# Pooling v on VectorE from a second load, with the first loads paced and the turns reordered

## The chip, the cores and the metric

The program runs on one core of one Trainium2 chip. The metric is the device time of one execution in microseconds (us). Engines are named as in the profile: PE is TensorE (PEld its weight loads), DVE is VectorE, ACT is ScalarE, POOL is GpSimd, SP is SyncE, whose queue issues all the loads.

## What is computed

Attention over q, k, v of shape (2, 8, 576, 64) in float32, and two MLPs behind it. The attention is a sum of two parts: a local one (each query sees the keys less than 4 positions away) and a pooled one, in which q, k and v are averaged over groups of 4 positions and the result is repeated 4 times.

```python
q_d = q.reshape(B, H, Sd, factor, D).mean(axis=3)      # k_d, v_d alike; Sd = 144
out_d = sm_attn(q_d, k_d, v_d)
out_up = np.repeat(out_d, factor, axis=2)
out_local = ...                                         # |i - j| < 4, softmax, times v
return out_up + out_local
```

The sum is laid out as 1152 tokens of 512 and goes through x @ w_in, a gate, @ w_out, and then through a mixture of 4 experts with a ReLU (w1, w2), weighted by domain_probs.

## The kernel before

**Units.** The attention runs in 8 units (`Unit`, u = 0 to 7): batch u // 4, and a pair of heads hp = u % 4, whose 2 x 64 dimensions lie on the 128 partitions. Two units share one slot for k and one for q (a pair of units, 0 to 3). All big buffers are slots of 128 x 2048 float32; there are 17 (`take`, `give`).

**Loads.** SP issues, in this order: k and q of unit 0, of unit 1, then v of batch 0 (`load_v`, nine loads), then k and q of units 2 and 3 (`load_qk(1)`). v is loaded as overlapping windows, so its 576 rows of 2048 B become 1091 rows. `load_qk(2)` follows in step 1. All else is in the list `later`, from which `load_next` takes one entry at its places in steps 2 and up: the halves of the first two w_in weights, v of batch 1, k and q of the last pair. Many of those wait for a one-element memset on DVE (`hold`), which itself waits for the slot.

**One unit's work.** `sums` adds groups of four of k and q (POOL; k of units 0 and 1 on DVE, L580). `pooled_scores` (four matmuls of 72 queries each, L670), `masks` (L594) and `scores` (L607) run on PE. `pooled_softmax`, `less_max`, `normalise` and `pooled_normalise` run on DVE, ACT and POOL. `turn` (L654) and `pooled_turn` (L724, eight transposes) turn the weights, ACT copies them to SBUF (`aT`, `aTd`). `values` multiplies by v in 72 local products (L744) and by the pooled v (L755), ACT copies the pooled part (`pd`), DVE adds it to the local part (`xf`, L769), ACT writes the high part of x (L777) and `low` the rest (DVE, L785).

**Pooled v.** `pool_v(b)` makes it with matmuls of v's windows against a matrix of ones (`fours`, L463), once for each batch: in step 1 for batch 0, behind 8 idle products, and in step 5 for batch 1. ACT copies the result into the last v slot (L471).

**Order.** The loop `for t in range(NU + 2)` (L1052) writes out the order of PE, DVE, ACT and POOL by hand; each engine works through its own list in order, and so SP through its own, whose order is not written by hand. Step t holds the scores of unit t, the turns of unit t - 1 and the values of unit t - 2. `idle_products` (L551) are matmuls on zeros whose result nobody reads: 4 ahead of `pooled_scores`, 4 ahead of `turn`. PSUM has three pairs of banks that go round (`banks()`) and one more pair (`banks(True)`), which the values use.

**Behind it.** `convert` takes one step at a time of the splitting of the MLP's weights: four steps a weight on DVE (L237, L247, L259 with L268, L226) with ACT between. In steps 8 and 9 the first products of the MLP (`pieces`, `first`, L374 to L376) mix with the last units. Piece f needs weight f // 2, all three of its products; the first piece with tokens of batch 1 needs x of unit 7 (`low`, L785).

## Time and profile before

| | us |
|---|---|
| median of 3 runs | 657.13 (656.95 to 657.19) |
| the profiled execution | 657.16 |
| its span, from the first to the last instruction | 655.0 |
| attention, until PE starts step 8 | 63.5 |
| its first 18.5 us, before PE starts step 2 | 18.5 |
| PE busy, of the span | 647.4 |
| DVE busy, of the span | 415.9 |

2.2 us of the profiled execution lie outside the span. Step t is counted from where PE starts its first idle products of that step.

### The profile page before, as it was taken

To read this page: it belongs to the slowest core of one execution; us is meant where nothing else is said; L and a number is where in the kernel's file an instruction comes from. 1 tells how busy PE (TensorE), PEld (TensorE's weight loads), DVE (VectorE), ACT (ScalarE), POOL (GpSimd) and SP (SyncE) were. 2 spreads that over 40 slices of the span, in tenths; PEclk is the share of its full clock that TensorE was granted. 3 is DMA by queue.
4 is the path that set the end of the run, shared out by engine and by line. 5 is a ranking of instruction groups with operands and counts; after the bars stand their busy time and mean duration, and the time that the engine had idled before them with its cause. 6 is when DMAs were issued, how large, how long until landed. Compare 5 with 4: busy or idle time off the path is not lost.

```text
span 655.0 us, 11972 instructions
## 1 busy us (share of the span) xinstructions
PE 647.4 (99%) x4929; PEld 582.6 (89%) x4943; DVE 415.9 (63%) x839; ACT 253.3 (39%) x591; POOL 95.3 (15%) x142
## 2 busy tenths in 40 slices
PE   8999999999999999999999999999999999999997
PEld 4657999999999999998998998998998988988985
DVE  6578899852794247585665665665765665755742
ACT  5567577442554246343233232241341331331410
POOL 4762000000000062101201201201201201201000
PEclk9999999999999999999999999999999999999999
DMA  8772333300510110300110110110210300200012
GB/s 278 226 236 91 130 124 134 129 1 1 193 66 1 65 64 1 131 2 0 65 65 1 65 65 1 65 65 1 87 43 0 129 2 15 115 1 2 2 48 97
DMA packets 12147, 45.89 MB, mean 70 GB/s; under 512 B 1334, under 2 KB 3382, under 8 KB 8252
## 3 DMA queue, kind: packets, MB, share of 16 engines
q1 hardware_dynamic: 12092, 45.12, 20.3%
q8 instruction: 39, 0.64, 0.4%
q14 instruction: 16, 0.13, 0.1%
HBM read 42.76 MB, written 2.36 MB: 69 GB/s over the span
## 4 chain that ended last, share of the span: by engine, by line
PE 96%; DMA 2%; SPq 1%; issue 0%; POOL 0%; DVE 0%; POOLq 0%
PE bank L936 27%; PE bank L1205 10%; PE bank L1206 10%; PE bank L1204 10%; PE bank L374 10%; PE bank L376 10%; PE bank L375 10%; PE pair L744 2%; PE pair L551 1%; DMA slot<-in_qT_dram 1%; PE pair L755 1%; DMA slot<-in_v_dram 1%; PE pair L607 1%; PE pair L724 1%; PE pair L670 1%; PE pair L654 1%
## 5 line engine op out<-in xcount | busy, mean ns | idle before, releaser
L936 PEld LDWEIGHTS bank<-xop,slot 128*128 128x128 f32 x1344 | 180.9, 188 | 1.3
L936 PE MATMUL bank<-xop,slot 128*128 128x288 f32 x1344 | 181.8, 295 | 0.0
L1205 PE MATMUL bank<-slot,h 128*128 128x512 f32 x288 | 113.9, 395 | 0.0
L1206 PE MATMUL bank<-slot,h 128*128 128x512 f32 x288 | 113.9, 395 | 0.0
L1204 PE MATMUL bank<-slot,h 128*128 128x512 f32 x288 | 113.8, 395 | 0.0
L1212 DVE SCALAR_TENSOR_TENSOR slot<-bank,pr,slot 128x512 f32<-128x512 f32 x63 | 47.3, 751 | 85.8 <-PE bank L1206 85.8
L442 POOL TENSOR_TENSOR st<-slot 128x256 f32<-128x256 f32 x16 | 13.9, 868 | 467.4 <-DMA slot<-in_w_dram 220.5
L1206 PEld LDWEIGHTS bank<-slot,h 128*128 128x128 f32 x288 | 54.1, 188 | 13.0
L1205 PEld LDWEIGHTS bank<-slot,h 128*128 128x128 f32 x288 | 54.1, 188 | 12.4
L1204 PEld LDWEIGHTS bank<-slot,h 128*128 128x128 f32 x288 | 54.1, 188 | 12.3
L376 PE MATMUL bank<-h,slot 128*128 128x384 f32 x192 | 64.7, 337 | 0.0
L375 PE MATMUL bank<-h,slot 128*128 128x384 f32 x192 | 64.7, 337 | 0.0
L374 PE MATMUL bank<-h,slot 128*128 128x384 f32 x192 | 64.7, 337 | 0.0
L374 PE MATMUL bank<-x,slot 128*128 128x384 f32 x188 | 63.1, 336 | 0.0
L376 PE MATMUL bank<-x,slot 128*128 128x384 f32 x188 | 62.9, 335 | 0.0
L375 PE MATMUL bank<-x,slot 128*128 128x384 f32 x188 | 62.9, 335 | 0.0
L442 DVE TENSOR_TENSOR u<-bank,u 128x288 f32<-128x288 f32 x96 | 43.6, 454 | 20.4 <-PE bank L936 20.0
L965 ACT ACTIVATE h<-c 128x288 fp32r<-128x288 f32 x64 | 27.9, 445 | 71.6 <-DVE c L442 71.5
L304 ACT ACTIVATE slot<-st 128x512 fp32r<-128x512 f32 x32 | 19.2, 624 | 64.6 <-POOL st L298 64.6
L825 DVE TENSOR_TENSOR h<-slot,h 128x384 fp32r<-128x384 f32 x48 | 27.5, 585 | 24.2 <-ACT h L824 24.1
L816 ACT ACTIVATE t<-bank,half__145 128x384 f32<-128x384 f32 x47 | 27.1, 581 | 40.1 <-PE bank L376 40.1
L817 DVE SCALAR_TENSOR_TENSOR slot<-t,bank 128x384 f32<-128x384 f32 x47 | 25.8, 552 | 24.5 <-ACT t L816 24.3
(115 smaller groups left out, 920.1 us busy)
## 6 DMA issues: line engine op xcount, KB each, us to landing
slot<-in_w_dram SPq DMA_DIRECT2D x16, 1024.0 KB, 4.8
slot<-in_w_out_dram SPq DMA_DIRECT2D x8, 1024.0 KB, 4.8
slot<-in_w_in_dram SPq DMA_DIRECT2D x6, 1024.0 KB, 5.3
slot<-in_v_dram SPq DMA_DIRECT2D x6, 512.0 KB, 4.8
out_dram<-slot SPq DMA_DIRECT2D x9, 256.0 KB, 2.0
slot<-in_w_in_dram SPq DMA_DIRECT2D x4, 512.0 KB, 5.9
slot<-in_kT_dram SPq DMA_DIRECT2D x3, 576.0 KB, 5.6
slot<-in_qT_dram SPq DMA_DIRECT2D x6, 288.0 KB, 6.0
```

Source lines behind the costliest of these rows:

```text
L374: nc.tensor.matmul(ps, wh, xh, start=first, stop=False)
L375: nc.tensor.matmul(ps, wh, xl, start=False, stop=False)
L376: nc.tensor.matmul(ps, wl, xh, start=False, stop=last)
L442: eng.tensor_tensor(out=out, in0=a, in1=b, op=ALU.add)
L816: nc.scalar.activation(out=t, in_=ps, func=AF.Relu, bias=half_, scale=1.0 / (6.0 * UP))
L825: nc.vector.tensor_tensor(out=g[:, 1, :], in0=u, in1=r32(g[:, 0, :]), op=ALU.subtract)
L936: nc.tensor.matmul(ps, a[:, i, k], b[:, j, k], start=start and k == 0 and n == 0, stop=stop and k == 1 and n == 2, skip_group_check=True,)
L965: nc.scalar.activation(out=self.h[:, 0, i, j], in_=of, func=AF.Relu)
L1204: nc.tensor.matmul(ps, hh, w[:, 0], start=(f == 0), stop=False)
L1205: nc.tensor.matmul(ps, hh, w[:, 1], start=False, stop=False)
L1206: nc.tensor.matmul(ps, hl, w[:, 0], start=False, stop=(f == NF - 1))
L1212: nc.vector.scalar_tensor_tensor(out=to, in0=ps, scalar=share, in1=to, op0=ALU.mult, op1=ALU.add)
```

## The change

Pooled v is no longer made on PE. A second load (`load_four`) brings v with four neighbouring rows on one partition, and DVE adds them: for each batch a part of 128 x 4 x 256, another of the same size (the other half of the columns), and one of 16 x 4 x 512. Each part takes two adds. Accordingly the rows of pooled keys are split 128 and 16 instead of 80 and 64, and the pooled queries of two heads are grouped in three groups (80 and 80 queries, and the last 64 of each head together), so that there are three exponentials instead of four and six transposes instead of eight.

The first loads go through `load`, which makes each wait for the load that lies 1.6 MB ahead of it, until about 5.9 MB are listed. k and q of units 2 and 3 now come ahead of v; the parts of pooled v follow v; k and q of the last pair come second and third in `later`, the pooled v of batch 1 behind v of batch 1.

In units 0 and 4 (`late`) the pooled values are multiplied one step later than the local ones: ACT copies the local part, and DVE adds the pooled one to it. In step t = 3 and t = 7 `pooled_turn` stands ahead of the pooled values. The sums of k of units 2 and 3 are made on DVE. Four idle products stand between the third and the fourth product of `pooled_scores`.

```diff
-KC = PK // 2
-KR = (80, 64)
+KR = (P, PK - P)
+QG = 80
+BY_DVE = 4
+FLY = 1_600_000
+FIRST_LOADS = (3 * 2 * 2 + 4 + 4) * S * P * 4 - 1
...
+    def load(out, in_):
+        size = math.prod(in_.shape) * 4
+        dma = nc.sync.dma_start(out=out, in_=in_)
+        if sum(n for _, n in flying) > FIRST_LOADS:
+            return
+        room = FLY
+        for ins, n in reversed(flying):
+            room -= n
+            if room < 0:
+                tc.add_manual_dep(dma.ins, ins.name, DONE, reason="loads on their way")
+                break
+        flying.append((dma.ins, size))
...
-    def pool_v(b, idle=0):
-        pool = banks(True)
-        idle_products(pool, idle)
...
-                    nc.tensor.matmul(
-                        pool[g * QB : g * QB + few, r, :],
-                        fours[rows, at : at + few],
...
+    def load_four(b, part):
+        if part == 0:
+            four_slots[b] = take(), take()
+        to, cols = four(b, part)
+        if b:
+            hold(to[:, 0])
+        src = v[b].rearrange("(p f) d -> p f d", f=FACTOR)
+        load(to, src[KR[0] * (part // 2) : KR[0] + KR[1] * (part // 2), :, cols])
+
+    def pool_v(b, part):
+        f4, cols = four(b, part)
+        add(nc.vector, f4[:, :2], f4[:, :2], f4[:, 2:])
+        add(nc.vector, pooled_v(b, part // 2)[:, cols], f4[:, 0], f4[:, 1])
...
     load_qk(0, 0, 1)
     load_qk(0, 1, 1)
+    load_qk(1)
     for p in range(NP):
         load_v(0, p)
-    load_qk(1)
+    for part in range(2):
+        load_four(0, part)
...
     later = [
         lambda: load_half(0, 0),
+        lambda: load_k(NU // 2 - 1, held=True),
+        lambda: load_q(NU // 2 - 1, held=True),
         lambda: load_half(0, 1),
         lambda: load_v(1, 0, (0,)),
         lambda: load_v(1, 0, (1,)),
         lambda: load_v(1, 1, (0,)),
         last_v,
-        lambda: load_k(NU // 2 - 1, held=True),
-        lambda: load_q(NU // 2 - 1, held=True),
+        lambda: load_four(1, 0),
+        last_four,
         lambda: load_half(1, 0),
         lambda: load_half(1, 1),
     ]
```

The new order of the steps, of which the old one stands in the kernel above:

```diff
+        elif t == 1:
+            n.pooled_scores(0, 4)
+            n.masks()
+            n.scores()
+            n.pooled_softmax()
+            units[0].pooled_normalise()
+            units[2].sums_q()
+            load_qk(2)
+            load_four(0, 2)
+            n.less_max()
+            n.normalise()
+            n.pooled_normalise()
+            for m in (2, 3):
+                units[m].sums_k()
+            units[3].sums_q()
+            units[0].turn(0)
+            units[0].pooled_turn()
+        elif t == 2:
+            n.masks(4)
+            n.scores()
+            n.pooled_scores(0)
+            n.less_max()
+            load_next(t)
+            n.pooled_softmax()
+            n.normalise()
+            load_next(t)
+            n.pooled_normalise()
+            pool_v(0, 0)
+            pool_v(0, 1)
+            load_next(t)
+            units[1].turn(4)
+            units[0].values()
+            units[1].pooled_turn()
+        elif t < NU:
+            n.pooled_scores(4)
+            n.masks()
+            n.scores()
+            n.pooled_softmax()
+            load_next(t)
+            n.less_max()
+            if t == NHP:
+                units[0].low()
+            if t > 3 and t != NHP + 3:
+                units[t - 3].low()
+            if t == 3:
+                units[4].sums()
+            if t % NHP == 3:
+                pool_v(t // NHP, 2)
+            if t == NHP + 2:
+                pool_v(1, 0)
+            n.pooled_normalise()
+            n.normalise()
+            load_next(t)
+            if t < NU - 2:
+                units[t + 2].sums()
+            units[t - 1].turn(4)
+            units[t - 2].values()
+            if t % NHP == 3:
+                units[t - 1].pooled_turn()
+            if not units[t - 2].late:
+                units[t - 2].pooled_values()
+            if t % NHP == 3:
+                units[t - 3].pooled_values()
+            else:
+                units[t - 1].pooled_turn()
+            if t == NHP + 2:
+                pool_v(1, 1)
+            convert((0, 1, 2, 1, 2)[t - 3])
+            load_next(t)
```

## Rows read from the trace of the kernel before

**Rows 1.** Page: busy time of each engine over the span
```profile
PE 647.4 (99%) x4929; PEld 582.6 (89%) x4943; DVE 415.9 (63%) x839; ACT 253.3 (39%) x591; POOL 95.3 (15%) x142
```
**Rows 2.** Page: the chain that ended last, by engine
```profile
PE 96%; DMA 2%; SPq 1%; issue 0%; POOL 0%; DVE 0%; POOLq 0%
```
**Rows 3.** Stretches: length, busy time (instructions) of each engine, granted clock, DMA, GB/s
```profile
0.00:7.70 7.70, 6.41 (x93) 3.00 (x95) 3.73 (x17) 3.68 (x5) 4.12 (x23) 1.00 0.71 203
7.70:18.46 10.76, 9.37 (x148) 4.40 (x149) 6.16 (x17) 5.08 (x21) 3.92 (x7) 1.00 1.01 336
...
25.66:32.75 7.09, 6.96 (x189) 4.70 (x189) 5.16 (x16) 4.17 (x15) 4.26 (x8) 1.00 0.69 220
32.75:39.50 6.75, 6.64 (x190) 4.52 (x189) 5.73 (x17) 5.30 (x17) 4.26 (x10) 1.00 0.77 255
39.50:49.72 10.22, 10.12 (x226) 5.55 (x225) 5.98 (x16) 5.36 (x17) 7.52 (x13) 1.00 0.75 232
49.72:56.76 7.04, 6.87 (x190) 4.62 (x189) 6.03 (x15) 5.21 (x17) 1.42 (x2) 1.00 0.51 175
56.76:63.47 6.71, 6.60 (x190) 4.49 (x189) 5.58 (x14) 5.17 (x17) 1.92 (x3) 1.00 0.02 5
...
77.30:120.00 42.70, 42.70 (x249) 42.70 (x248) 42.15 (x78) 28.24 (x54) 0.00 (x0) 1.00 0.38 134
120.00:270.00 150.00, 150.00 (x859) 150.00 (x858) 86.64 (x151) 65.44 (x129) 16.92 (x16) 1.00 0.16 57
```
**Rows 4.** Timeline, start-up: start, length, engine, line, operation, idle before and releaser
```profile
11.62 0.56 PE L654 MATMUL pair<-ident,ex 64*128 64x64 f32 x10 [0.75 <-POOL ex L640]
...
16.95 1.31 POOL L442 TENSOR_TENSOR slot<-slot 128x288 f32<-128x288 f32 x3 [3.78 <-DMA slot<-in_kT_dram]
...
18.65 1.17 POOL L442 TENSOR_TENSOR slot<-slot 128x288 f32<-128x288 f32 x2 [0.39 <-DMA slot<-in_qT_dram]
...
19.88 0.71 PE L670 MATMUL pair<-slot 64*72 64x144 f32 x8 [0.38 <-POOL slot L442]
```
**Rows 5.** Timeline, PE in one whole step (t = 3)
```profile
25.66 1.03 PE L551 MATMUL pair<-zeros 128*128 128x512 bf16 x3
26.62 0.71 PE L670 MATMUL pair<-slot 64*72 64x144 f32 x8
...
29.79 1.35 PE L744 MATMUL pair<-aT,slot 38*64 38x32 f32 x72
31.08 1.21 PE L755 MATMUL pair<-aTd,slot 80*64 80x144 f32 x8
32.22 0.70 PE L724 MATMUL pair<-ident,exd 72*80 72x72 f32 x8
```
**Rows 6.** Timeline, PE: the pooling of v of batch 1 in step 5
```profile
42.06 3.64 PE L463 MATMUL pair<-slot,fours 38*32 38x512 f32 x36
```
**Rows 7.** Groups by line and shape, DVE until 78 us: count, busy, mean ns
```profile
L785 DVE TENSOR_TENSOR x<-xf,x 128x576 fp32r<-128x576 f32 x8 | 6.1, 768 | 0.2 <-ACT x L777 0.2
L683 DVE TENSOR_REDUCE mxd<-pair 72x4 f32<-72x576 f32 x8 | 5.9, 742 | 6.6 <-PE pair L670 6.5
...
L769 DVE TENSOR_TENSOR xf<-pair,pd 128x256 f32<-128x256 f32 x8 | 3.3, 415 | 0.0
...
L226 DVE TENSOR_TENSOR slot<-slot 128x512 fp32r<-128x512 f32 x4 | 2.6, 685 | 0.2 <-ACT slot L221 0.2
```
**Rows 8.** Timeline, steps 8 and 9: what the MLP's first products need from DVE
```profile
72.79 1.29 DVE L226 TENSOR_TENSOR slot<-slot 128x512 fp32r<-128x512 f32 x2 [0.18 <-ACT slot L221]
...
73.65 0.34 PE L376 MATMUL bank<-x,slot 128*128 128x384 f32 x1
...
76.98 1.42 DVE L785 TENSOR_TENSOR x<-xf,x 128x576 fp32r<-128x576 f32 x2
```
**Rows 9.** Timeline, POOL: the sums of one unit, twice
```profile
26.05 2.44 POOL L442 TENSOR_TENSOR slot<-slot 128x288 f32<-128x288 f32 x5
...
33.06 2.77 POOL L442 TENSOR_TENSOR slot<-slot 128x288 f32<-128x288 f32 x5
```
**Rows 10.** Timeline, PE: the first idle products
```profile
1.29 4.85 PE L551 MATMUL pair<-zeros 128*128 128x512 bf16 x11 [1.29 <-DVE zeros L484]
```

## What the change should do to the time

> **What bounds the kernel now.** I read the page's first part, the chain of waits, and then a table of stretches cut at the steps. PE is busy for 647 of 655 us [rows 1] and 96% of the chain that ends last is PE [rows 2]; so time is won only by taking work off PE or by closing the few places where it waits. From 77.3 us on PE has no idle time [rows 3], and the change touches nothing there. What counts is when PE reaches the first product that no unit is mixed with, at 77.3 us; behind it I take the remaining 577.7 us as they are.
>
> Two regimes lie before that. Until 18.5 us PE's work is thin and the loads run at their limit: 336 GB/s with the DMA engines full [rows 3]. POOL waits 3.8 us for k and again for q of units 2 and 3, and the pooled scores of unit 2 start at 19.88 right behind that [rows 4]. From 25.7 us on PE is over 97% busy in each step. A step takes 7.09, 6.75, 7.04 and 6.71 us, but step 5 takes 10.22 [rows 3], since the pooling of v sits in it for 3.64 us [rows 6]. DVE is at 73 to 86% in these steps, 59% in step 5 [rows 3]: off the path, but the next to come.
>
> **Start-up.** By the rates of rows 3, 7.7 us x 203 GB/s = 1.56 MB have moved at 7.7 us, and 0.336 MB per us follow. k and q of a unit are 0.59 MB (2 x 128 x 576 x 4 B), v's windows 1091 x 2048 B = 2.23 MB. Before, k of units 2 and 3 was in at 16.95 us [rows 4], when 1.56 + 9.25 x 0.336 = 4.67 MB had moved, though only 4.0 MB stood up to it in the list: a load is done when some 0.7 MB behind it have moved too. In the new list k and q of four units end at 2.36 MB, thus at 10.1 us, or 12.2 with those 0.7 MB. v ends at 4.59 MB: 16.7 to 18.8. The two big parts of pooled v end at 5.64 MB: 19.8 to 21.9. k and q of the third pair end at 6.82 MB, 23.4 to 25.5, and the small part of pooled v at 6.95 MB, 23.7 to 25.8.
>
> PE then goes so. `turn(0)` at 11.6 us as before [rows 4], waiting for POOL; POOL's pooled product of unit 0 lets `pooled_turn(0)` run at 12.6 to 13.2. Step 2: four idle products 0.9, masks and scores 1.1 (15.2); the pooled scores need the sums of q (POOL) and k (DVE), which stand behind unit 1's softmax: ready at about 15.2, so 15.9; idle products and `turn(1)` 1.5 (17.4). The 72 local products take 1.3 [rows 5] and wait for v: between 17.4 and 18.8. With `pooled_turn(1)`, 0.6, step 3 starts at 19.3 to 20.7. Step 3: 1.6 for idle products and pooled scores, 1.1 for masks and scores, 1.5 for idle and turn, 1.3 values, 0.6 pooled turn, then the pooled values of two units, 0.8 each [rows 5]: 27.1 at the earliest. The latest end comes from DVE's queue: 23.0 with the last big part of pooled v, unit 3's two maxima and its subtraction 1.6, the small part (in at 25.8) 1.9, so the pooled values begin at 27.8 and step 4 at 29.4; with one more us for loads that were listed later and issued earlier, 30.5. I take 28.4, in the middle, where before step 4 began at 32.75: **-4.4 us (-5.7 to -2.3)**. The work moved here has its cover: four adds on DVE in a stage where it was half idle.
>
> **Steps 4 to 7.** Pooling of batch 1 leaves PE: step 5 falls from 10.22 to the mean of the other three, 6.83, which is **-3.4 us**. Six transposes for eight move the same 576 columns, and two adjacent pooled products now share a head, so that I take the rest of PE's work as equal (within 0.3 us for all units). One pooled value moves from step 6 to step 7.
>
> What DVE gets in place of this has no row. The nearest are two-input operations on SBUF: 128 x 512 take 0.685 us, and 128 x 256 take 0.415 (one input in PSUM) [rows 7]. So a big part costs 0.69 + 0.42 = 1.1 us, and the small one, 1024 and 512 columns on 16 partitions, about 1.3 + 0.7 = 2.0: 4.2 us a batch, or 3.7 at the least, as neighbouring instructions overlap by some 0.08 us. Batch 1 has its 4.2 in steps 6 and 7, and there stand also two conversion steps instead of one in 5 and 7, and one add for unit 4; the maximum over three groups instead of four gives back 0.2 a step. Against 5.6 to 6.0 us before [rows 3], DVE then has about 6.8 in step 5, 6.9 in step 6 and 8.9 in step 7, while PE has 20.5 in the three: DVE falls behind by 2 us more. The small part for batch 1 then ends at about step 7 + 6.4 us where PE wants it at + 5.9 (0.5 lost), and the low part of the first weight, which stands behind it, comes about 1.2 us late for the first product of step 8. In the old kernel such things were already just in time: the low part of the second weight began at 72.79 and its first user ran at 73.65; x of unit 7 was complete at 78.4, with its first user's group starting at 77.3 [rows 8]. So I charge **+1.8 us (0 to +4)**; zero if DVE overlaps well, 4 if POOL's sums and the loads hold it up too.
>
> The Trainium skill speaks against this part: "SBUF — State Buffer", section "Who interferes with whom", says that a DVE instruction with two SBUF inputs and a GpSimd instruction that reads SBUF block each other for a whole instruction. The trace has POOL's same five adds at 2.44 and at 2.77 us [rows 9], a difference of 0.3 which agrees in sign. By the rule, the six adds a batch could each wait for one POOL add of 0.5 us (a fifth of 2.44); all of it would be 3 us, on DVE. I do not add it to the sum; my upper bound covers it.
>
> ACT loses two copies of pooled v a batch and one exponential a unit, and gains the copies of units 0 and 4: hidden, as it was at 79% or less in each step [rows 3]. SP now issues three more loads a batch; those of batch 1 are due in step 6, and at 0.336 MB per us the 12.5 MB listed up to there are in by 40 us, a little ahead of it.
>
> **The sum.** Against the profiled execution, 657.16 (span 655.0 and 2.2 around it; 0.03 above the median): -4.4 - 3.4 + 1.8 = -6.0. **I predict 651.2 us.**
>
> **Rivals.**
> *Loads not better (654.5).* SP's order is not written by hand, and the pace binds only the first 5.9 MB: q of the third pair and parts of v of batch 1 may be issued ahead of what is needed. Then v and pooled v are in 3 to 4 us later, the start-up gives about 1 us in place of 4.4, and 657.1 - 1 - 3.4 + 1.8 = 654.5. For it: loads are done some 0.7 MB late already. Against: k and q of four units need only 2.36 MB, whatever follows.
>
> *DVE becomes the bound (654).* If its adds wait for POOL or cost twice my rows, DVE falls 4 to 5 us behind by step 8, and the stall takes 4.7: 654.0. It can't take much more: behind step 9 DVE is ahead by whole weights and stays busy at 99% until 120 us without holding PE, and at 58% after it [rows 3].
>
> *DVE blocked on a load (slower, 660).* The adds of pooled v stand in DVE's queue ahead of the normalisation of units 3 and up, and everything on PE follows. Step 4 starts some 3.5 us behind the landing of the small part. If that part shares the queue with 4 MB issued without a pace (weights, v of batch 1, the last pair), it lands at 23.7 + 12 = 36 us, step 4 starts at 39.5 instead of 32.75, and 657.1 + 6.7 - 3.4 = 660.4; the turning point is a landing at 32.6 us. Against: loads before were late by 0.7 MB, not by 4.
>
> *A slow clock in the start-up (655).* The first idle products took 0.44 us each at the start [rows 10], and 0.24 later (four from 25.66 to 26.62) [rows 5], though the granted clock reads 1.00 in both: the first fits 1.2 GHz, the second 2.4. The new order has fewer idle products before 18 us and a wait for v. If PE falls to the lower rate there, steps 2 and 3 lose up to 4 us: 655. Against: a wait of 0.75 us [rows 4] changed nothing. "TensorE: Matmul & The Clock Gate", Part 1 in the Trainium skill, says that the slow rate is the default and activity lifts it; no row shows the rate falling again.
>
> **How the numbers follow.** The forecast has 0.62, loads not better 0.13, DVE the bound 0.12, a slow clock 0.04, blocked on a load 0.09. The forecast's own range is -5.7 - 3.4 + 0 - 0.3 = -9.4 at best, 647.8, and -2.3 - 3.4 + 4 at worst, 655.4. Taken with the rivals on the same side, 647.8 to 655.0 holds about 8 in 10. A measurement of this kernel can tell about 0.2%, 1.3 us, from no change. Faster by more than that: 0.62 + 0.12 + 0.12 + 0.02 = 0.88; the same 0.04; slower 0.08.
>
> **What the new profile would show.** Right: pooled scores of unit 2 at 15 to 16 us; step 4 from 28 to 29; steps 4 to 7 of 27 to 28 us in all without products in the middle of step 5; PE waiting for DVE (the small part of pooled v, the first weight) 1 to 3 us around step 8; the first unmixed product at about 71.3. Wrong: PE waiting for v or for the sums beyond 20 us, DVE waiting for the load of pooled v, DVE's adds far from 1.1 and 2.0 us, or PE's idle products above 0.3 us after 10 us. The forecast falls if step 4 starts after 31, or if PE's waits on DVE between steps 5 and 9 exceed 4 us.

## The result and the profile after

The changed kernel takes 663.40 us (median of 10 runs, 662.04 to 668.10), the kernel before 657.31 beside it: the ratio is 1.0103 (95% interval 1.0075 to 1.013). The forecast was 651.2 with a range of 647.8 to 655.0, so it missed in sign and by 12 us. Three of the ten runs, the profiled one (668.1) among them, lie at 667.6 to 668.1 with a mean granted clock of 0.979 or 0.980, the other seven at 662.0 to 664.5 with 0.982 to 0.987, so that the trace shown here lies 4.7 us above the median; one run each of E3, E9 and E10, more than 1.5% above the fastest of its kernel, is left out of the table below.

The page of the changed kernel, where rows of before are [rows 1, 2]; PEclk is the granted clock in 40 slices of the span, and all 40 were 9 before:

```profile
PE 654.3 (98%) x4847; PEld 586.3 (88%) x4847; DVE 423.2 (64%) x852; ACT 250.7 (38%) x575; POOL 92.0 (14%) x127
...
PEclk9889599999999999999999999999999999999999
...
PE 94%; DMA 4%; SPq 1%; DVE 1%; issue 1%; ACT 0%; ACTq 0%
```

PE has fewer instructions than before (4847 for 4929) and is busy longer (654.3 for 647.4). The second, third and fifth slice say why: the clock is below its upper level in part of each. The stretches, cut at the steps, answer [rows 3] (length, busy time and instructions of PE, PEld, DVE, ACT, POOL, granted clock, DMA share, GB/s):

```profile
0.00:7.70 7.70, 6.37 (x93) 3.05 (x93) 4.20 (x18) 3.69 (x5) 3.37 (x18) 1.00 0.69 224
7.70:18.40 10.70, 9.97 (x252) 6.25 (x250) 8.76 (x25) 6.37 (x26) 6.64 (x13) 1.00 0.90 283
18.40:33.66 15.26, 12.00 (x226) 6.82 (x224) 8.31 (x21) 5.33 (x18) 5.84 (x10) 0.84 1.03 317
33.66:43.72 10.06, 9.79 (x189) 5.52 (x187) 6.62 (x18) 4.20 (x13) 4.46 (x7) 0.73 0.47 141
43.72:51.16 7.44, 7.44 (x188) 4.69 (x187) 4.29 (x16) 5.04 (x15) 3.98 (x8) 1.00 0.76 222
51.16:58.22 7.06, 6.89 (x179) 4.43 (x179) 6.82 (x16) 4.01 (x14) 3.29 (x4) 1.00 0.56 179
58.22:68.90 10.68, 9.60 (x195) 5.60 (x194) 9.27 (x19) 5.27 (x17) 3.82 (x4) 0.88 0.51 189
68.90:85.96 17.06, 15.76 (x202) 13.10 (x200) 9.44 (x17) 8.20 (x17) 0.00 (x0) 0.57 0.19 63
85.96:120.00 34.04, 34.04 (x198) 34.04 (x197) 33.30 (x62) 22.17 (x42) 0.00 (x0) 1.00 0.36 124
```

The rows are: the start, step 2 with the end of step 1, step 3 with the last products of step 2 (from the wait for v on), then steps 4, 5, 6, 7, then steps 8 and 9, then the MLP. Step 4 begins at 33.66 (before 32.75), the first product of step 8 at 68.90 (before 63.47), and the first product behind the last unit at 85.96 (before 73.19). From there 580.4 us follow, before 581.8. So 12.8 us are lost up to that point, 1.4 come back behind it, and the spans (666.3 and 655.0) differ by 11.3. Steps 5 and 6, at full clock, take 7.44 and 7.06 us, where whole steps without the pooling took 6.71 to 7.09.

The same view in finer stretches shows where the clock went; 0.5 is 1.2 GHz, 1.0 is 2.4 GHz:

```profile
22.50:25.00 2.50, 2.50 (x8) 0.72 (x6) 1.54 (x4) 0.00 (x0) 0.00 (x0) 0.50 1.08 370
...
32.00:38.00 6.00, 6.00 (x26) 2.31 (x26) 3.55 (x10) 1.83 (x4) 4.18 (x6) 0.52 0.41 105
...
40.00:64.00 24.00, 23.03 (x579) 14.75 (x578) 19.83 (x50) 13.27 (x42) 10.98 (x14) 1.00 0.70 229
...
66.00:82.00 16.00, 14.70 (x134) 11.01 (x132) 9.35 (x21) 6.84 (x16) 1.69 (x2) 0.51 0.03 5
```

And these are PE's waits behind 18 us (timeline: start, length, engine, line, operation, count, and in brackets the idle time before it and what ended it):

```profile
19.88 0.98 PE L770 MATMUL pair<-aT,slot 38*64 38x32 f32 x24 [1.48 <-DMA slot<-in_v_dram]
31.89 1.84 PE L796 MATMUL pair<-aTd,slot 16*64 16x144 f32 x12 [1.79 <-DVE slot L470]
41.91 0.43 PE L770 MATMUL pair<-aT,slot 38*64 38x32 f32 x12 [0.27 <-issue]
57.34 0.30 PE L770 MATMUL pair<-aT,slot 38*64 38x32 f32 x3 [0.17 <-issue]
64.55 1.11 PE L770 MATMUL pair<-aT,slot 38*64 38x32 f32 x54 [1.08 <-issue]
71.21 0.69 PE L389 MATMUL pair<-x,slot 128*128 128x384 f32 x1 [1.30 <-DVE slot L239]
```

Each of the three stretches at half clock (from 22.0, 32.2 and 66.3 us) begins 0.3 to 2.1 us behind the end of a wait of PE: that for v (1.48), that for the small part of pooled v (1.79), and that marked issue at 63.5 to 64.6 (1.08). The last one goes on to 83 us, with another wait (1.30, the low part of the first weight) in it. What PE loses there is not the 1 to 2 us of a wait but what follows: steps 8 and 9 take 17.06 - 1.30 = 15.8 us without the wait in them, against 9.7 before.

DVE's rows behind two of these waits, the additions of pooled v and the order in which step 7 ends:

```profile
21.78 1.15 DVE L470 TENSOR_TENSOR slot<-slot 128x512 f32<-128x512 f32 x2 [2.55 <-DMA slot<-in_v_dram]
29.79 2.04 DVE L470 TENSOR_TENSOR slot<-slot 16x1024 f32<-16x1024 f32 x2 [2.33 <-DMA slot<-in_v_dram]
...
68.05 0.82 DVE L812 TENSOR_TENSOR xf<-pair,pd 128x320 f32<-128x320 f32 x2 [0.90 <-ACT pd L804]
69.80 0.76 DVE L470 TENSOR_TENSOR xf<-xf,pd 128x576 f32<-128x576 f32 x1 [0.93 <-ACT pd L804]
70.47 1.28 DVE L239 TENSOR_TENSOR slot<-slot 128x512 fp32r<-128x512 f32 x2
```

The small part of pooled v lands at 29.8; DVE itself waits 2.33 us for it. The low part (L239) stands behind two additions of x that each wait for ACT's copy of the pooled values.

### The profile page after: what moved, and what is told of

Its sections match the earlier page's. It is cut to its first block, busy times and chain, and to the rows that moved or that the text cites. A ratio compares the mean times of both kernels' runs of the same rounds, so it can differ in the third digit from the quotient of the medians.

```text
span 666.3 us, 11796 instructions
## 1 busy us (share of the span) xinstructions
PE 654.3 (98%) x4847; PEld 586.3 (88%) x4847; DVE 423.2 (64%) x852; ACT 250.7 (38%) x575; POOL 92.0 (14%) x127
## 4 chain that ended last, share of the span: by engine, by line
PE 94%; DMA 4%; SPq 1%; DVE 1%; issue 1%; ACT 0%; ACTq 0%
PE bank L979 27%; PE bank L1298 10%; PE bank L1299 10%; PE bank L1300 10%; PE bank L387 10%; PE bank L389 10%; PE bank L388 10%; DMA slot<-in_v_dram 2%; PE pair L770 1%; PE pair L563 1%; DMA slot<-in_qT_dram 1%; PE pair L796 1%; PE pair L699 1%; SPq L398 1%; PE pair L755 1%
## 5 line engine op out<-in xcount | busy, mean ns | idle before, releaser
L470 POOL TENSOR_TENSOR st<-slot 128x256 f32<-128x256 f32 x16 | 13.7, 858 | 474.5 <-DVE slot L322 206.5
L387 PE MATMUL bank<-x,slot 128*128 128x384 f32 x188 | 64.0, 340 | 0.0
L389 PE MATMUL bank<-x,slot 128*128 128x384 f32 x188 | 63.6, 338 | 0.0
L388 PE MATMUL bank<-x,slot 128*128 128x384 f32 x188 | 63.6, 338 | 0.0
L470 DVE TENSOR_TENSOR u<-bank,u 128x288 f32<-128x288 f32 x96 | 43.5, 453 | 20.2 <-PE bank L979 19.7
L860 DVE SCALAR_TENSOR_TENSOR slot<-t,bank 128x384 f32<-128x384 f32 x47 | 25.8, 552 | 25.1 <-ACT t L859 25.0
```

Source lines behind the costliest of these rows:

```text
L387: nc.tensor.matmul(ps, wh, xh, start=first, stop=False)
L388: nc.tensor.matmul(ps, wh, xl, start=False, stop=False)
L389: nc.tensor.matmul(ps, wl, xh, start=False, stop=last)
L470: eng.tensor_tensor(out=out, in0=a, in1=b, op=ALU.add)
```

## The experiments

One figure serves all of them. A span times (1 - its mean granted clock) is what the clock takes, if PE sets the time throughout; each run lists both numbers, the clock to three places (so 0.3 us of rounding). Each column has the median of its own values over the runs (before: all 130 runs beside E1 to E18), so a row need not add up; the ratio is that of the comparison, not the quotient of the medians:

| kernel | time | ratio to before | taken by the clock | time less that |
|---|---|---|---|---|
| before | 657.30 | | 0.3 | 657.0 |
| changed | 663.40 | 1.0103 [1.0075, 1.013] | 9.3 | 653.8 |
| E1 idle products at the waits | 664.12 | 1.0097 [1.0069, 1.0125] | 7.6 | 657.1 |
| E2 before, heads in a row | 657.59 | 1.0000 [0.9985, 1.0015] | 0.3 | 656.9 |
| E3 small part loaded early | 661.48 | 1.0067 [1.0043, 1.009] | 8.6 | 652.5 |
| E4 before, no idle products | 661.62 | 1.0041 [1.0017, 1.0066] | 14.2 | 646.1 |
| E5 conversion first | 661.98 | 1.0077 [1.0046, 1.0109] | 8.6 | 653.4 |
| E6 E1 + E3 + E5 | 662.84 | 1.0065 [1.0039, 1.009] | 6.0 | 657.4 |
| E7 before, batch 1 on DVE | 659.53 | 1.0028 [1.001, 1.0045] | 3.3 | 655.7 |
| E8 E6, narrow products together | 659.20 | 1.0040 [1.002, 1.006] | 3.3 | 655.7 |
| E9 before, loads only | 659.05 | 1.0003 [0.9977, 1.0029] | 0.7 | 657.5 |
| E10 E8, lows later | 657.77 | 1.0034 [0.9997, 1.007] | 2.6 | 655.2 |
| E11 E10, loads paced 0.7 MB | 658.70 | 1.0017 [0.9985, 1.0049] | 3.3 | 655.2 |
| E12 E7, loads paced 0.7 MB | 665.34 | 1.0107 [1.0055, 1.016] | 8.3 | 657.2 |
| E13 E10, loads paced 1.2 MB | 660.02 | 1.0028 [1.0007, 1.0049] | 4.3 | 654.9 |
| E14 E13, additions later | 659.34 | 1.0016 [0.9982, 1.005] | 3.9 | 655.7 |
| E15 E10, additions later | 660.36 | 1.0039 [1.0018, 1.006] | 4.0 | 655.5 |
| E16 before, one late low part | 659.85 | 1.0039 [1.0023, 1.0055] | 1.0 | 659.0 |
| E17 E10 without added idle products | 660.47 | 1.0029 [1.0006, 1.0052] | 9.5 | 650.6 |
| E18 E10, idle products in start-up only | 658.98 | 1.0005 [0.9982, 1.0029] | 5.9 | 653.1 |

### Is it the clock? E1, E4

E1 puts 20 idle products where the changed kernel's PE waits.

```diff
-        def values(self):
+        def values(self, idle=0):
             pv = self.pv = banks(True)
+            idle_products(pv, idle)
...
-        def pooled_turn(self):
+        def pooled_turn(self, idle=0):
             tr = banks()
+            idle_products(tr, idle)
...
-            units[0].values()
+            units[0].values(6)
...
-                units[t - 1].pooled_turn()
+                units[t - 1].pooled_turn(8 if t == 3 else 6)
```

> The changed kernel with 20 more idle products on PE (about 4.8 us of work at 0.24 us each): 6 ahead of the 72 local products of unit 0 in step 2, 8 ahead of the pooled turn in step 3, 6 ahead of the one in step 7. Theory A (the clock: PE falls to the lower rate after each of its waits, and that costs some 8 us): the granted clock stays above 0.995 and the time falls from 663.4 to 653 to 657. Theory B (added work and waits alone make the change slower, the clock costs little): the time stays at 662 or rises to as much as 668, as there is more work on PE.

The half clock of the start-up is gone (1.00 up to 54 us), and step 4 begins at 31.6 instead of 33.66, 1.6 of it because the small part of pooled v landed at 28.2 instead of 29.8 in this run. But the time does not fall; 664.12 lies where theory B had it. The wait for the low part of the first weight is 2.26 us now, and the clock is at 0.5 from 54 to 58 and from 68 to 78.

```profile
52.44 0.54 PE L772 MATMUL pair<-aT,slot 38*64 38x32 f32 x16 [0.23 <-issue]
...
67.35 0.45 PE L389 MATMUL pair<-x,slot 128*128 128x384 f32 x1 [2.26 <-DVE slot L239]
```

So with idle products in the waits the clock stays up there, and it falls at other places: behind the long wait, but also 1.9 us behind a wait of only 0.23. E4 is the other side of it: the kernel before without the idle products of steps 1 to 7.

```diff
-                n.pooled_scores(4)
+                n.pooled_scores(0)
...
-            units[t - 1].turn(0 if t in (1, NU) else 4)
+            units[t - 1].turn(0)
```

> The kernel before without the idle products of steps 1 to 7 (4 ahead of the pooled scores and 4 ahead of the turn in each; those of step 0 and of the pooling of batch 0 stay). Theory A (clock): the gaps that open slow PE; the granted clock falls below 0.98 and the time rises above 657.3, though some 12 us of work are gone from PE. Theory B: the time falls by 3 to 10 us with the work, and the clock stays at 0.99 or more.

```profile
26.92 0.35 PE L607 MATMUL pair<-slot 64*32 64x38 f32 x26 [0.44 <-issue]
...
29.00:42.00 13.00, 13.00 (x264) 9.44 (x263) 9.73 (x26) 7.62 (x24) 8.27 (x14) 0.50 0.65 201
...
49.50:53.00 3.50, 3.50 (x90) 2.56 (x90) 3.08 (x6) 2.54 (x6) 0.57 (x2) 0.51 0.96 383
...
56.30:59.80 3.50, 3.50 (x104) 2.63 (x104) 3.46 (x7) 2.60 (x6) 1.17 (x2) 0.51 0.02 5
```

Some 11 us of PE's work are gone (646.1 without what the clock takes), and the clock takes 14.2 back (some 10 in the profiled run, which took 655.93): PE is busy in every one of these stretches, and still at half clock. Ahead of the first stands a wait of only 0.44 us (marked issue, up to 26.92). The long wait is thus not all that counts; how dense PE's work is counts too. In the kernel before the idle products pay for themselves.

### The pooled products: E2, E8

The prediction took the pooled products as equal. They are not. Before, a set takes 0.71 us [rows 5], 0.65 by the starts (26.62 to the masks at 27.27); in the changed kernel, in step 5 at full clock, three products and, behind four idle products, the fourth:

```profile
43.72 0.90 PE L699 MATMUL pair<-slot 64*64 64x144 f32 x6
44.55 1.04 PE L563 MATMUL pair<-zeros 128*128 128x512 bf16 x4
45.52 0.46 PE L699 MATMUL pair<-slot 64*64 64x144 f32 x2
```

By the starts this is 0.83 + 0.39 = 1.22 us a unit. E2 swaps two loops in the kernel before, so that neighbours share a head as in the changed kernel.

```diff
-            for qh in range(2):
-                for h in range(2):
+            for h in range(2):
+                for qh in range(2):
                     d = slice(h * D, (h + 1) * D)
```

> The kernel before with the two loops of its pooled products swapped: both products of one head, then both of the other, so that neighbours share the rows of the array, as they do in the changed kernel. Theory P (the order of heads makes the pooled products longer): each set of four takes 1.0 to 1.3 us instead of 0.65 to 0.71, and the kernel 657.3 + 2 to 4.5 us. Theory Q (their length comes from the wider shapes or from the idle products between them): 0.65 to 0.75 us as before, and the time within 0.7 us of 657.3.

Nothing changes (0.72 a set): with 72 columns each, heads in a row are not the cause. The trace of the changed kernel has a gap of 0.2 us on PEld between the weights of the 64-column product and of the 128-column ones behind it:

```profile
51.54 0.30 PEld L699 LDWEIGHTS pair<-slot 64*128 64x128 f32 x4 [0.20 <-issue]
```

E8 puts the two with 64 columns next to each other.

```diff
-                (1, 0, slice(0, D), QG),
                 (0, 0, slice(0, P), 0),
                 (2, 1, slice(0, P), 0),
+                (1, 0, slice(0, D), QG),
                 (1, 1, slice(D, P), QG),
...
-                if idle and len(made) == 3:
+                if idle and len(made) == 2:
```

> As the run with all three things, and the four pooled products of a unit in another order: the two with 128 query columns first, the two with 64 columns next to each other, the idle products between the pairs. Theory S (the pooled products take 1.25 us a unit instead of 0.71 because PE stops for about 0.2 us at each change between a 64-column and a 128-column stationary operand): the set takes 0.2 to 0.3 us less in each of units 2 to 7, 1.2 to 2 us less than the run with all three. Rival (each of these products is longer, whatever its neighbour): no difference.

```profile
45.66 0.52 PE L699 MATMUL pair<-slot 64*128 64x144 f32 x4
46.11 1.04 PE L563 MATMUL pair<-zeros 128*128 128x512 bf16 x3
47.08 0.46 PE L699 MATMUL pair<-slot 64*64 64x144 f32 x4
```

The two pairs take 0.45 and 0.40 us by the starts of what follows them, 0.85 a unit: 0.37 less for the same products in another order (a whole step falls from 7.44 to 7.06). The time falls by 3.6 us against E6, but by the table only 1.7 of it is work, as the 1.2 to 2 expected; the rest is the clock. The rows also say where the 0.37 lies. Each product has two records. One product with 64 columns by itself takes 0.46 us (x2, at 45.52 in the changed kernel), and two next to each other take the same 0.46 (x4, at 47.08 in E8): side by side in place of one after the other. So a 64-column product beside 128-column ones runs alone, and that is what costs; the gap on PEld that I took for the cause is part of it, and no run tells how large a part.

### DVE's queue and the small part: E3, E5, E6, E10

E3 loads the small part of pooled v right behind the big ones, ahead of the third pair.

```diff
-    for part in range(2):
+    for part in range(3):
         load_four(0, part)
...
-            load_four(0, 2)
```

> The changed kernel with the small part of pooled v of batch 0 (16 partitions) loaded right behind the two big ones instead of behind k and q of the third pair. The load is then in at about 24 us instead of 29.8. Theory A (clock): PE's wait of 1.8 us at 30 us goes, and with it the stretch at half clock from 32 to 38 us: 663.4 falls to about 658, the granted clock rises by 0.009. Theory B (waits alone): 661.6, the clock as it was.

DVE's addition no longer waits for it (25.80, 2.18 us long), and PE waits elsewhere, 1.85 us, for nothing the profile names; from 26 to 40 us the clock is at 0.5, and again at 71 to 81. The time, 661.48, is the one of theory B (661.6), but the stretch at half clock did not go as theory A asked, it moved: this run does not decide between the two.

```profile
26.38 2.34 PE L770 MATMUL pair<-aT,slot 38*64 38x32 f32 x72 [1.85 <-issue]
```

E5 moves the low part of the first weight ahead of the additions of x.

```diff
+            if t == NU - 1:
+                convert(2)
             if not units[t - 2].late:
                 units[t - 2].pooled_values()
...
-            convert((0, 1, 2, 1, 2)[t - 3])
+            convert((0, 1, 2, 1, 0)[t - 3])
```

> The changed kernel with one move: in the last step with a unit (t = 7) the two conversion steps, the low part of the first weight among them, stand ahead of the additions of x of units 5 and 4 in DVE's queue. Theory D (the first product of step 8 waits because the low part stands behind two additions that wait for ACT): PE no longer waits for line L239 (1.30 us in the changed kernel, 2.3 in two other runs), the half-clock stretch at 66 to 83 us is gone, and 4 to 6 us with it: 657 to 660. Rival, density (the clock falls in steps 7 and 8 whatever PE waits for, since their products are small): the wait goes, the half clock stays, 661 to 663.

PE's wait for L239 is gone and the half clock at that place is short (67 to 71 us, behind a wait of 0.81 marked issue), nearly as theory D had it; but the profile has a wait of 2.49 us marked issue at 26 to 28.5 and half clock from 30 to 40, and the time is 661.98, as the rival had it. E6, the lines of E1, E3 and E5 together:

> The changed kernel with three things at once: the small part of pooled v loaded right behind the two big parts, six to eight idle products at the three places where PE was seen to wait in the start-up, and the conversion steps of t = 7 ahead of the additions. Theory A (the loss is the clock, which falls after PE's waits): no stretch at half clock after 12 us, step 4 from about 31, 652 to 656. Rival, density: one or two stretches at half clock stay somewhere in 26 to 80 us, 658 to 662.

No wait over 1 us is left behind 13 us, and there are still three short stretches at half clock (29 to 32, 56 to 59, 73 to 76), the second with no wait over 0.25 us in the 29 us ahead of it. That is what the rival about density expected, not theory A. With 20 idle products and the long pooled products the time is no better. E10, on top of E8, moves two low parts of x behind the gate of the first MLP product in DVE's queue.

```diff
-                units[t - 4].low()
-                units[t - 3].low()
                 pieces(1, banks()[:, 0, :TC])
+                units[t - 4].low()
+                units[t - 3].low()
```

> As the run with the narrow products together, and in step 8 the low parts of x of units 4 and 5 stand behind the first MLP product's gate in DVE's queue instead of ahead of it. Theory D (the wait of 0.66 to 0.98 us for line L862 in step 8 is the order of DVE's queue, and the half clock behind it goes with it): that wait under 0.2, no half clock at 70 to 74, 1.5 to 3 us less than that run: 656 to 657.7. Rival: the wait moves to x of units 4 and 5 and the time stays at 659.

The wait for L862 falls from 0.66 to 0.28 us and the half clock at 70 to 74 is gone; the gain is 1.4 us by the medians, just under the 1.5 to 3 expected and, by the ratios (1.0040 and 1.0034), not clear of the scatter. A half-clock stretch at 53 to 57 is left, behind a wait of 0.71 marked issue.

### Waits marked issue: E7, E9

These waits stand apart by a number. In the changed kernel 256 records of PE and PEld lie between those that end at 57.34 and at 64.55, and three times as many (765 recorded) between 41.91 and 57.34:

```profile
41.91:57.34 15.43, 15.26 (x383) 9.64 (x382) 11.74 (x32) 8.76 (x28) 8.85 (x12) 1.00 0.63 189
57.34:64.55 7.21, 6.13 (x128) 3.66 (x128) 6.83 (x16) 3.89 (x14) 2.14 (x2) 1.00 0.79 290
```

And the DMA view has one packet of the instruction queue (38 in all, 0.62 MB, so 16 KB each) 62.27 to 63.21 us, 1.3 us ahead of the end of the second wait; between 57.4 and 62.2 there is none. The queues between 62.2 and 63.3 us (packets, MB, share of 16 engines):

```profile
q1 hardware_dynamic: 52, 0.37, 83.4%
q8 instruction: 1, 0.02, 5.3%
```

In all the traces, between 12 and 100 us, every wait of PE of 0.3 us and more that is marked issue ends 1.2 to 1.6 us behind the end of such a packet. PE waits for the next block of its own instructions. Behind the wait that ends at 57.34 the next packet starts 4.9 us later (the data queue takes 85% of the DMA engines in between), behind the one that ends at 64.55 it starts 1.1 us later (engines free). The Trainium skill, "Runtime: NRT & Kernel Launch", section "Instruction fetch mechanics", says that an engine fetches its instructions in blocks of 16 KiB, 256 instructions, over a DMA queue of its own, and that this is mostly hidden. The trace agrees with the block; hidden it is not here, where 256 records of small products last 4 to 7 us and the loads fill the DMA engines.

E7 is the kernel before with one part of the change: DVE pools batch 1 from a second load.

```diff
+    def load_four(part):
+        four_slots.append(take())
+        to = four_slots[part][0].rearrange("p (f d) -> p f d", f=FACTOR)[: KR[part]]
+        hold(to[:, 0])
+        src = v[1].rearrange("(p f) d -> p f d", f=FACTOR)
+        at = part * KR[0]
+        nc.sync.dma_start(out=to, in_=src[at : at + KR[part]])
+    def add_four(part):
+        ...
+        add(nc.vector, f4[:, :2], f4[:, :2], f4[:, 2:])
+        add(nc.vector, pooled_v(1, part), f4[:, 0], f4[:, 1])
...
         lambda: load_q(NU // 2 - 1, held=True),
+        lambda: load_four(0),
+        lambda: load_four(1),
...
-        if t == NHP + 1:
-            pool_v(1)
+        if t == NHP + 2:
+            add_four(1)
...
+        if t == NHP + 1:
+            add_four(0)
```

> The kernel before with one part of the change alone: v of batch 1 is pooled by DVE (four additions) from a second load, the 36 products of L463 in step 5 and two copies on ACT are gone; batch 0, keys of 80 and 64, loads and their order are as before. Theory B (the pooling costs PE 3.64 us and nothing takes its place): 653.5 to 654.5, the span of steps 4 to 7 shorter by 3.0 to 3.6 us, no half clock. Rival, DVE: its four additions in steps 5 and 6 (4 us) make PE wait for x or for the first weight, and the clock falls there: 656 to 660.

```profile
53.58 1.06 PE L758 MATMUL pair<-aT,slot 38*64 38x32 f32 x54 [1.92 <-issue]
56.53 0.75 PE L769 MATMUL pair<-aTd,slot 64*64 64x144 f32 x4 [1.49 <-DVE slot L442]
```

Up to step 5 the 3.4 us are won: the masks of unit 6 begin at 48.6 instead of 51.3, though step 4 began 0.7 us late. Then PE waits 1.92 us for its instructions and 1.49 for DVE, whose second addition came behind that, and is at half clock from 55 to 62. The part of the change that was surest to gain ends slower (1.0028). E9 separates the loads from DVE: the two loads are made and nobody reads them; PE still pools.

```diff
+        slot = take()
+        to = slot[0].rearrange("p (f d) -> p f d", f=FACTOR)[: KR[part]]
+        ...
+        nc.sync.dma_start(out=to, in_=src[at : at + KR[part]])
+        give(slot)
```

> The kernel before with two more loads and nothing else: the rows of v of batch 1 that the other run pooled from (640 and 512 KB) are loaded into free slots at the end of steps 4 and 5, and nobody reads them; TensorE still pools v itself. Theory I (PE's idle time marked issue is PE waiting for a block of its own instructions, whose load queues behind data loads on the DMA engines; such waits stand 256 records apart): PE waits of 0.5 to 2 us marked issue appear between 40 and 60 us, at the end of an instruction load, the granted clock halves behind them, 659 to 661. Rival (the loads are hidden, the losses of the run with batch 1 on DVE came from DVE alone): 656.5 to 658, no such wait.

```profile
55.05 0.26 PE L616 MATMUL pair<-slot 64*32 64x38 f32 x4 [0.31 <-issue]
62.21 0.77 PE L616 MATMUL pair<-slot 64*32 64x38 f32 x65 [0.73 <-issue]
66.21 0.65 PE L753 MATMUL pair<-aT,slot 38*64 38x32 f32 x23 [0.88 <-issue]
```

The waits are there, 255 records apart, with no change in DVE's or PE's work. What they cost is not clear: the profiled run took 663.2, the median is 659.05 beside 657.06, and the interval (0.9977 to 1.0029) holds 1. The mechanism is shown; its price in the kernel before differs from run to run, and the 659 to 661 that I expected is not shown.

### Pace and order: E11 to E15

E11 lets every load of the attention stage behind the first 5.9 MB wait until no more than 0.7 MB ahead of it are on their way (on top of E10); E13 the same with 1.2 MB, E12 with 0.7 MB on top of E7.

```diff
-        if sum(n for _, n in flying) > FIRST_LOADS:
+        if sum(n for _, n in flying) > ALL_LOADS:
             return
-        room = FLY
+        room = FLY if sum(n for _, n in flying) <= FIRST_LOADS else LATE
```

> As the run before it, and all loads of the attention stage behind the first 5.9 MB, the weights' too, wait until no more than 0.7 MB ahead of them are on their way. Theory I (blocks of PE's instructions come late because they queue behind data): no PE wait marked issue over 0.4 us behind 12 us, no half clock, 652.5 to 655.5. Rival pace: the loads themselves come late, PE, DVE or POOL waits for k, q, v or the weights, 657 or more. Rival density: no waits, but the clock falls all the same, 657 or more.

> As the run of the kernel before with batch 1 pooled by DVE, and every load behind the first 4 MB waits until no more than 0.7 MB ahead of it are on their way. Theory I: the waits marked issue (0.76 and 1.92 us) go, the wait of 1.49 us for DVE behind the second goes with it, no half clock: 653.5 to 655.5, and the 3.4 us that the prediction gave for taking the pooling off PE show. Rival DVE (its four additions hold PE up): a wait for DVE over 1 us and half clock behind it stay, 657 to 660.

> As the paced run, with 1.2 MB instead of 0.7 MB on their way. Theory L (at 0.7 MB the loads of batch 1 come late: VectorE waits 0.85 and 0.56 us for them in step 6, and PE 2.37 us for VectorE in step 7): these waits go, PE's wait for line L644 falls under 1 us, 654 to 656.5. Rival V (VectorE's queue is too full in steps 6 and 7 whatever the loads do): a wait of PE for VectorE over 1.5 us stays, 657 to 659.

In E11 one wait marked issue is left over 0.4 us (0.55 at 24.9), and PE reaches the masks of unit 7 at 52.7, where it was 58.4 before and 60.4 in the changed kernel. Then 2.37 us are lost at one place:

```profile
58.96 2.43 PE L565 MATMUL pair<-zeros 128*128 128x512 bf16 x5 [2.37 <-DVE ex L644]
```

DVE had waited 0.85 and 0.56 us for the paced loads of batch 1, so its softmax of unit 7 was late. The rival about pace was right there, and wholly so in E12, where POOL's sums come late (PE waits 1.85 and 1.62 us for them) and DVE's second addition holds PE up for 3.49. At 1.2 MB (E13) the wait for DVE is gone, as theory L had it, and a wait of 1.60 for instructions is back at 53.5 to 55.1; the time is 660.02, not 654 to 656.5. Neither value is good: the same DMA engines carry the loads and the instructions.

E14 (on E13) and E15 (on E10) move additions of batch 1 behind the normalisations in DVE's queue.

```diff
-            if t % NHP == 3:
-                pool_v(t // NHP, 2)
-            if t == NHP + 2:
-                pool_v(1, 0)
+            if t == 3:
+                pool_v(0, 2)
             n.pooled_normalise()
             n.normalise()
+            if t == NU - 1:
+                pool_v(1, 2)
+            if t == NHP + 2:
+                pool_v(1, 0)
```

> As the run paced at 1.2 MB, and in steps 6 and 7 the first additions of pooled v of batch 1 stand behind the two normalisations in VectorE's queue instead of ahead of them. Theory V (the additions block the softmax that the next turn waits for): 1 to 3 us less than the run paced at 1.2 MB, PE without a wait for VectorE over 0.7 us in steps 6 and 7, 652.5 to 655.5. Rival L (the loads decide): no difference.

> As the run with the lows later, without the pace of late loads, and with the additions of batch 1 behind the normalisations as in the run with the adds later. Theory I (instruction blocks late behind data): waits marked issue of 0.3 to 1.3 us stay at 25 to 27 and at 50 to 60 us and one of them still halves the clock; 656 to 659, 1.5 us or more above the paced run. Rival: the order in VectorE's queue was all, and this run is as fast as the paced one.

PE now waits 1.76 us for the small part of batch 1 itself (line L472 in E14, L470 in E15). The order isn't the matter: ahead of the normalisation the addition delays the turn (E11), behind it the pooled values. DVE has too much to do in step 7, as the prediction's sum had it, though that alone does not make the loss. E15 also keeps its instruction waits (1.28 at 26.6 to 27.9, half clock behind it from 30), as theory I expected; the two differ by less than their scatter.

### One wait, and the idle products: E16, E17, E18

E16 leaves PE's instructions and all loads of the kernel before as they are; only the low part of the first weight is made a step later.

```diff
-        convert(3 if t >= NU else 2 if t == 3 else 1 if t > 3 else 0)
+        convert(4 if t == NU else 3 if t > NU else 2 if t == 3 else 1 if t in (4, 5, 7) else 0)
```

> The kernel before with TensorE's instructions and all loads unchanged: only the low part of the first weight is made by VectorE one step later, behind the additions of x of unit 5, so that the third product of step 8 waits for it about 1.0 us (VectorE would begin it at 64.2, its first half is there at 64.9, PE wants it at 63.9). Theory A (a wait of this size ahead of step 8 halves the clock for a stretch): the granted clock is 0.5 for 3 to 14 us behind 66 us, 659.5 to 664. Rival (a wait costs its own length): no half clock, 658 to 658.6.

```profile
65.31 0.44 PE L376 MATMUL pair<-x,slot 128*128 128x384 f32 x1 [0.88 <-DVE slot L226]
```

The wait is 0.88 us (about 1.0 was worked out), and the profiled run has no half clock at all behind it: a wait of this size, with dense products behind, does not have to take the clock down. Five of the ten runs have a mean clock of 1.00 and take 658.5 to 659.4, 1.2 to 2.1 above the kernel before; the other five have 0.995 to 0.997 and take 660.3 to 662.4. So the same program goes either way, and theory A in the sharp form that I gave it falls. (Not all five need be the wait's doing: 23 of the 130 runs of the kernel before have 0.997 or less too.) Longer waits also passed at full clock:

```profile
15.86 2.79 PE L463 MATMUL pair<-slot,fours 38*16 38x512 f32 x28 [1.42 <-DMA slot<-in_v_dram]
26.61 0.46 PE L671 MATMUL pair<-ident,ex 64*128 64x64 f32 x6 [1.09 <-issue]
```

The first is in E16, with the pooling right behind it, the second in E10. A wait is a chance of losing the clock, not a certainty, and what else decides it no run separates.

E17 takes the 20 added idle products out of E10, E18 only the six of step 7.

```diff
-            units[0].values(6)
+            units[0].values()
...
-                units[t - 1].pooled_turn(8 if t == 3 else 6)
+                units[t - 1].pooled_turn()
```

> As the run with the lows later, without the 20 added idle products. Theory A (idle products pay by the clock): less what the clock takes, 650.5 to 652.5, as 20 products of 0.26 us are gone in places where TensorE waits anyway in part; the clock takes 5 to 9 us again, so 657 to 660 in all. Rival (the waits that lowered the clock are mended by the other changes, and the idle products are ballast): the clock takes 3 us or less and the time is 653 to 655.5.

> As the run with the lows later, without the six added idle products of step 7; the 14 of the start-up stay. Theory A: 1 to 1.6 us less work for TensorE, the clock loses as much or more in steps 7 and 8: 657.5 to 660. Rival: 656 to 657, since TensorE waits for VectorE in step 7 anyway and the first stretches of step 8 are dense.

```profile
59.57 1.11 PE L770 MATMUL pair<-aT,slot 38*64 38x32 f32 x54 [2.29 <-issue]
```

E17 without what the clock takes is 650.6, and the clock takes 9.5: nearly as theory A had it, 0.5 more for the clock and for the time. Against E10 the 20 idle products are 4.6 us of work and save 6.9 of the clock; by the ratios (1.0029 and 1.0034) the two kernels are level. One wait of 2.29 us for instructions is in the profile, half clock from 61 to 68 behind it. E18 lies between (653.1 and 5.9), within theory A's range, and ends level with the kernel before (1.0005, 0.9982 to 1.0029), by the ratio the best of all the variants of the change. None beats the kernel before.

## Why the prediction was wrong

**The clock** is the step that failed. The prediction gave it 0.04, a place in steps 2 and 3 and 4 us, with the argument that a wait of 0.75 us had changed nothing [rows 4] and no row shows the rate falling again. That was true of one trace whose waits were both short; it is no evidence on waits of 1 to 2 us. The forecast itself held two such waits (PE for v, and 1 to 3 us for DVE around step 8) and charged them at their length. By the table the clock takes 9.3 us in the median run, and what is left, 653.8, lies in the forecast's range; E17, with some of the waits mended, is 650.6 without its clock, beside a forecast of 651.2. What is shown is that the clock fell and what it took; that waits bring it down is shown in part only: in the changed kernel each fall stands behind one, but E1, E4 and E6 have falls behind 0.2 to 0.4 us, and E10 and E16 longer waits without a fall. The Trainium skill, "TensorE: Matmul & The Clock Gate", Part 1, puts the cost of the ramp under 1% of a typical span. Here the clock takes 9.3 of 663.4 us, 1.4%, on a kernel whose PE is 98% busy, and not by one ramp at the start but by three falls.

**Start-up.** Right: the pooled scores of unit 2 run at 14.83 (15 to 16 was forecast), since k and q stand ahead of v, and DVE's big parts cost 1.15 us (1.1) and the small one 1.92 to 2.04 (2.0). Wrong: v is complete at 20.5 instead of 16.7 to 18.8, and the small part at 29.8 instead of 23.7 to 25.8. Two terms failed. The first is the rate, taken as 0.336 MB per us from the kernel before: from 7.7 to 18.4 us it was 283 GB/s, from there 317. By these rows 5.4 MB had moved at 20.5, 0.8 more than the 4.59 up to v, so for v the rate alone was wrong. Whether the pace of 1.6 MB lowered it, no run tells. The second is "a load is done when some 0.7 MB behind it have moved too": at the landing of the small part 8.4 MB had moved, 1.4 more than the 6.95 listed up to it. SP issued it at 21.46, behind k of the third pair, which SP could issue only at 19.90, and in the 8.3 us to its landing 317 GB/s moved 2.6 MB, the first weight and pair 4 among them. So the pooled values that need it began at 31.89 where 27.8 was the latest end, and step 4 at 33.66: the forecast falls by its own mark (after 31). (The 0.8 that the prediction reads for a unit's pooled values in rows 5 stands there as 1.21; in the other steps of the kernel before it is 0.86, so this did no harm.) The turning point of the rival "blocked on a load", a landing at 32.6, was not reached; its 660 was nearer in size than in mechanism.

**Steps 4 to 7.** The pooling did leave PE: no product of it stands in step 5. But "the rest of PE's work as equal (within 0.3 us for all units)" was 1.22 - 0.65 = 0.57 us a unit too low, by the starts, 4.6 us over eight: more than the 3.4 of the pooling that was saved here. E8 shows that 0.37 of it is the order of narrow and wide operands. The row was there to be doubted: 64 x 144 with 72 columns [rows 5] was taken for 64 and 128 columns.

**DVE.** The term of +1.8 was about right: the low part of the first weight came 1.30 us late (1.2 was forecast), DVE was busy for 9.3 us in step 7 (8.9), and E14, E15 and E11 show that the small part of batch 1 or the softmax of unit 7 is late by 1.8 to 2.4 us as soon as the rest is mended. Of the wait of DVE for POOL, which the prediction left out of its sum, the trace has a sign: of the two big parts of batch 1 the second, with POOL at work beside it, takes 0.77 us more, and POOL's normalisation, 0.82 us at 50.25, takes 1.27.

```profile
56.68 1.14 DVE L470 TENSOR_TENSOR slot<-slot 128x512 f32<-128x512 f32 x2
58.86 1.91 DVE L470 TENSOR_TENSOR slot<-slot 128x512 f32<-128x512 f32 x2
...
59.22 1.27 POOL L657 TENSOR_TENSOR ex<-ex,rec 128x380 f32<-128x380 f32 x1
```

That PE's waits for DVE lie just ahead of long work at half clock was not in the price.

**What the prediction did not have at all:** more loads delay PE's instructions (E7, E9). It counted SP's loads as hidden when they landed in time for their readers.

The sum, in the profiled run against the forecast: start-up 33.66 - 28.4 = 5.3, mostly the late small part; steps 4 to 7 35.2 - 27.3 = 7.9, of which 2.3 are pooled products, 1.5 waits marked issue, and 4.0 the clock (10.06 x 0.27 and 10.68 x 0.12); steps 8 and 9 17.1 - 9.7 = 7.3, of which 1.3 is the wait for the low part and 6.0 the clock. The DVE term of 1.8 was in the forecast already and goes off, and so do 1.4 us behind the last unit, of which no run tells the cause: 17.3. Around the span lie 1.8 us instead of 2.2: 16.9, and the profiled run is 668.1 - 651.2 = 16.9 above the forecast.

## What to carry to other kernels

Where PE's products are small, price a wait of PE not at its length but with the stretch at half clock that may follow, and look for what keeps the clock up before taking dense work off PE: without its idle products the kernel before had less work and took longer (E4). Whether the pooling's own products held the clock up too, no run shows. Count a new load against everything that shares the DMA engines, the engines' own instructions included, not only against its reader. And two products of equal size are equal only in the same neighbourhood of operand shapes.

## What the hardware showed that was not expected

- PE waits for its own instructions: 16 KB blocks of 256 records, the next one asked for, as it looks, when PE enters the one before; 1.1 to 2.1 us to the start of the load with the DMA engines under 30% busy, up to 5.3 (E5) with full ones, then about 1 us for the load and 1.2 to 1.6 us until PE goes on.
- The granted clock falls in the middle of a kernel whose PE is 98% busy. Ahead of it stood waits of 0.2 us (E1) to 2.5 us (E5); a wait of 0.88 us was followed by half clock in E9's trace and not in E16's, and one of 1.42 us left it up (E16).
- Two products with 64 columns of the stationary operand (64 rows each, two heads) take 0.46 us next to each other, as long as one alone; beside products with 128 columns each of them ran alone (E8).
